# Batch 0: the second state of heads 4 to 7 formed once, and earlier

## The chip, the cores and the metric

The kernel runs on one core of a Trainium2 chip. The metric is the device time of one launch in microseconds, as a median of several runs. A separate execution is recorded by the hardware profiler; its times are those quoted from the profile and the trace.

## The reference

Eight batches of eight heads, 576 positions, head size 64, go through a causal linear attention with a decay for each head (retention); its output of 4608 rows x 512 goes through a feed-forward layer of width 2048 whose activation is h * sigmoid(beta * h).

```python
scores = (1.0 / np.sqrt(D_)) * np.matmul(q, k.transpose(0, 1, 3, 2))
gamma = 1.0 - 2.0 ** (-5.0 - np.arange(H))
Dmat = np.where(rel >= 0, gamma[:, None, None] ** rel[None, :, :], 0.0)   # rel = row - column
ret = np.matmul(scores * Dmat[None], v)
x = ret.transpose(0, 2, 1, 3).reshape(B * S, H * D)
h = x @ w_in
out = (h * (1.0 / (1.0 + np.exp(-beta * h)))) @ w_out
```

The inputs and the output are float32; the matmuls work on bfloat16 copies.

## The kernel before

**Work and tiles.** The first 512 positions of each batch are one block; the last 64 positions of all eight batches together are a ninth block. For each block the attention gives xT, the output transposed (channels on the partitions), then `up` or `ups` forms the 16 pieces of the hidden layer (four matmuls of 128x512 each, and a Silu on ACT into gT), and `down` forms the output rows (16 matmuls of 128x512 for each of four row groups).

**Attention by pieces and states.** The decay is split into a gain on the queries and one on the keys' side, so that within a piece of positions the masked scores times the values give the output, and what comes from earlier pieces is a product of the queries with a state, the sum of keys times values (128x128 for a pair of heads, of which the two 64x64 diagonal blocks count). The matmuls of queries with a state are called cross products.

**Batch 0.** Its 512 positions lie in two spans of 256 (s = 0, 1), each of two pieces of 128: a span's partitions 0 to 63 hold its first piece (`low`) and 64 to 127 its second (`high`). Heads are handled in two halves: a = 0 is heads 0 to 3, a = 1 is heads 4 to 7. The steps are:

- `pre_s`: casts or scales keys and values of a span and a half, on POOL.
- `s_T`: four transposes of the keys (line 470) into a PSUM tile T, and a copy of it by ACT into kT (line 471).
- `s_sc`: 16 score matmuls of 64x64 weights (line 486), then two masks on DVE (line 489) that write R.
- `s_O`: 16 matmuls of R with the values (line 500) into two PSUM tiles of outputs, one for each parity of the piece.
- `s_st(a, n, s, rows, at, fresh)`: state matmuls over the given rows of span s for half a, into bank n of two PSUM banks (tiles `st`). It takes either eight matmuls of 64x64 (line 525) or four of whole pairs of heads (line 531).
- `s_keep(a, n, es, bank, at)`: two casts of a state (lines 540, 542) into `sbds[n]`, the state ahead of piece n + 1, by the engines es. n = 3 keeps the last state in `ends[0]`.
- `s_cross(c, a)`: two cross products of piece c with `sbds[c - 1]` (line 508).
- `s_x(a, hh, e)`: copies one tile of outputs into xT on engine e (line 512).

For heads 4 to 7 the state of span 0 is formed twice, once in each bank: bank 1 becomes the second state and bank 0 is continued with the low rows of span 1 to become the third.

`keep_warm` is a filler: one 128x512 matmul whose result nobody reads. `warm_up` is the same at the start.

**Order.** The kernel's schedule is by hand: each engine executes its instructions in the order in which the program writes them, and semaphores are set by the framework from the tiles that are read and written, for PSUM by whole banks. Slots of a PSUM tag (`mm` 3, `O` 2, `sc` 2, `st` 1) are taken from those that are free.

Ahead of the large products stand the calls of lines 763 to 819. Then `merged` goes through `fill`, a list of large products, and calls the steps of the other streams at the positions in that list that they are given: `rest` (the cross products of heads 4 to 7 and the copies of their outputs) at 1, after the first four products; `last_products` at 2.5; `last_state` at 3.6. Fill's first item is the first half of two hidden pieces, which needs the outputs of heads 0 to 3; its third item needs those of heads 4 to 7.

**Batch 1** works in pieces of 128 too, one step for each (i = 4 to 7): `a_O` outputs, `a_st` state matmuls, `a_cross` cross products, `a_x` the copies to xT, `a_keep` the copies of a state. `second(4)` does these for pieces 4 and 5 near the end of batch 0's `down`. For i = 5 the output lies in two banks, one copied by DVE (line 421), the other by ACT (line 422).

DMAs are issued by SP in the order of the program; the first ones are the queries, keys and values of batch 0, and then the weights. None of the steps that the change touches issues one.

Of the kernel before, what the change touches and what calls it, by code (L numbers as in the profile page):

```python
# [19 lines left out]
def kernel(  # L20
# [10 lines left out]
    nc = tc.nc  # L31
    B, H, S, D = q.shape
# [213 lines left out]
    def keep_warm(tag="mm"):  # L246
        ph = psum.tile([P, CB, P], F32, name="ph", tag=tag, bufs=3 if tag == "mm" else 1)
        nc.tensor.matmul(ph[:], ident[:], ident[:].unsqueeze(1).to_broadcast([P, CB, P]), start=True, stop=True,  # L248
                         skip_group_check=True)
# [16 lines left out]
    def xt(m):  # L266
        if m not in xts:
            xts[m] = xpool.tile([P, HP, CB, P], BF16, name="xT", tag="xT" if m < B else "xTt", bufs=2 if m < B else 1)
        return xts[m]
# [9 lines left out]
    def head_of(b, p, j):  # L279
        return 2 * p + (j if b is not None and b < QB or p < 2 else 1 - j)  # L280
# [49 lines left out]
    def heads(t, p):  # L330
        return t[:, 2 * p:2 * p + 2, :].rearrange("p h d -> p (h d)")
# [27 lines left out]
    def q_cols(i, r, p):  # L359

        b, c = seq[i]
        if b is None:
            return live[i]["qkT"][r, 0, p, :], lambda o: o
        return (batch[b]["qT"][r, :, p, c * PC:(c + 1) * PC], lambda o: o.rearrange("k (i s) -> k i s", i=CB))
# [20 lines left out]
    def new_O(i):  # L385
        tags = ("O", "sc") if split(i) else ("O",)
        live[i]["O"] = [psum.tile([P, 2 if split(i) else HP, P], F32, name="O", tag=t, bufs=2) for t in tags]

    def O_of(i, p):
        Os = live[i]["O"]  # L390
        return Os[p // 2][:, p % 2] if split(i) else Os[0][:, p]

    def opens(i, p):
        return p == 0 or split(i) and p == 2

    def a_cross(i):

        b, c = seq[i]
        for p in range(HP):
            for j in range(2):  # L400
                rhs, view = q_cols(i, half(j), p)
                nc.tensor.matmul(view(O_of(i, p)[half(head_of(b, p, j) % 2)]), sbq[2 * c - 1][half(j), p, :], rhs,
                                 start=False, stop=True, skip_group_check=True)

    def a_O(i):

        b, c = seq[i]
        L = live[i]
        new_O(i)
        R, vn = L["R"], L["vn"]  # L410
        for j, p in [(n % 2, n // 2) for n in range(H)]:
            h = head_of(b, p, j)
            nc.tensor.matmul(O_of(i, p)[half(h % 2)], vn[:, h, :], R[:, j, p, :],
                             start=opens(i, p), stop=c == 0, skip_group_check=True)

    def a_x(i):
        b, c = seq[i]
        x, view = xt(b)[:, :, :, c * PC:(c + 1) * PC], lambda o: o.rearrange("k p (i s) -> k p i s", i=CB)
        Os = live[i]["O"]
        if split(i):  # L420
            nc.vector.tensor_copy(x[:, :2], view(Os[0]))
            nc.scalar.copy(x[:, 2:], view(Os[1]))
        else:
            (nc.scalar.copy if i < E + 2 else nc.vector.tensor_copy)(x, view(Os[0]))

    def a_st(i):

        b, c = seq[i]
        L = live[i]
        if c == 0:  # L430
            state_ps[b] = psum.tile([P, HP, D], F32, name="st", tag="st", bufs=1)
        for p in range(HP):
            for j in range(2):
                nc.tensor.matmul(state_ps[b][half(j), p, :], L["kn"][:, 2 * p + j, :], L["vn"][:, head_of(b, p, j), :],
                                 start=c == 0 and p == 0, stop=True, skip_group_check=True)

    def a_keep(i):

        b, c = seq[i]
        nc.scalar.copy(sbq[2 * c + 1][:], state_ps[b][:])  # L440
        if c:
            nc.vector.tensor_copy(sums[c % 2][:], state_ps[b][:])
# [3 lines left out]
    def half(x):  # L446
        return slice(x * D, (x + 1) * D)

    act, dve = nc.scalar.copy, nc.vector.tensor_copy
# [15 lines left out]
    def s_T(s, a):  # L465
        S = spans[s]
        T = psum.tile([P, 2, 2, P], BF16, name="T", tag="O", bufs=2)
        for i in range(2):
            for pl in range(2):
                nc.tensor.transpose(T[:, i, pl, :], heads(S["kn"][:, i], 2 * a + pl), ident[:])  # L470
        act(S["kT"][:, :, 2 * a:2 * a + 2], T[:])  # L471

    def s_q(c, r, p):
        return batch[0]["qT"][r, :, p, c * PC:(c + 1) * PC]

    def s_view(o):
        return o.rearrange("k (i s) -> k i s", i=CB)
# [13 lines left out]
    s_Os, s_sts = {}, {}  # L491

    def s_O(s, a, tag):

        if s == 0:
            s_Os[a] = [psum.tile([P, 2, 2, P], F32, name="O", tag=tag, bufs=2) for _ in range(2)]
        for i in range(2):
            for pl in range(2):
                for j, hh in spread:
                    nc.tensor.matmul(s_Os[a][hh][half(j), s, pl, :], spans[s]["vn"][half(hh), i, 2 * (2 * a + pl) + j, :],  # L500
                                     spans[s]["R"][a][half(hh), j, i, pl, :], start=s == 0 and i == 0 and pl == 0,
                                     stop=i == 1 and s == 0 and hh == 0, skip_group_check=True)

    def s_cross(c, a):

        for pl in range(2):
            p = 2 * a + pl
            nc.tensor.matmul(s_view(s_Os[a][c % 2][:, c // 2, pl, :]), sbds[c - 1][:, p, :], s_q(c, slice(0, P), p),
                             start=False, stop=True, skip_group_check=True)

    def s_x(a, hh, e):
        e(xt(0)[:, 2 * a:2 * a + 2].rearrange("k p i (s h w) -> k (p i) s h w", s=2, h=2)[:, :, :, hh, :],
          s_Os[a][hh].rearrange("k s p (i w) -> k (p i) s w", i=CB))

    def s_st(a, n, s, rows, at=None, fresh=False):

        if n not in s_sts:
            s_sts[n] = psum.tile([P, HP, P], F32, name="st", tag="mm" if n else "st", bufs=3 if n else 1)
            fresh = True
        S, at = spans[s], 2 * a if at is None else at  # L520
        if a == 0 and rows != whole_span:
            for i in range(2):
                for p in range(2):
                    for j in range(2):
                        nc.tensor.matmul(s_sts[n][half(j), at + p, half(j)], S["kn"][rows, i, 2 * p + j, :],
                                         S["vn"][rows, i, 2 * p + j, :], start=fresh and i == 0 and p == 0, stop=True,
                                         skip_group_check=True)
            return
        for i in range(2):
            for p in range(2):  # L530
                nc.tensor.matmul(s_sts[n][:, at + p, :], heads(S["kn"][rows, i], 2 * a + p), heads(S["vn"][rows, i], 2 * a + p),  # L531
                                 start=fresh and i == 0 and p == 0, stop=True, skip_group_check=True)

    def s_keep(a, n, es, bank=None, at=None):

        ps, at = slice(2 * a, 2 * a + 2), 2 * a if at is None else at
        for j in range(2):
            st = s_sts[min(n, 1) if bank is None else bank][half(j), at:at + 2, half(j)]
            if n < 3:
                es[j](sbds[n][half(j), ps, half(j)], st)  # L540
            else:
                es[j](ends[0][half(1 - j if a else j), ps], st)
# [220 lines left out]
    whole_span, low, high = slice(0, P), half(0), half(1)  # L763
# [11 lines left out]
    keep_warm()  # L775
    pre_s(0, 0, 0)
    s_T(0, 0)
    pre_s(1, 0, 0)
    keep_warm()
    s_sc(0, 0, "sc")  # L780
    s_T(1, 0)
    pre_s(0, 0, 1)
# [17 lines left out]
    s_st(0, 1, 1, low)  # L800
    s_keep(0, 2, (act, act))
    s_O(1, 0, "O")
    s_cross(1, 0)
    s_cross(2, 0)
    s_x(0, 0, act)
    s_cross(3, 0)
    s_x(0, 1, act)
    s_st(1, 1, 0, whole_span)
    s_st(1, 0, 0, whole_span, 0, True)
    s_st(1, 0, 0, low)  # L810
    s_st(1, 0, 1, low, 0)
    s_keep(1, 1, (dve, dve))
    s_keep(1, 0, (dve, dve))
    s_keep(1, 2, (act, act), 0, 0)
    s_O(0, 1, "sc")
    s_O(1, 1, "sc")
    cast_w_in(0, (0, 1), (1,))
# [9 lines left out]
        nc.vector.reciprocal(rbeta_sb[:], beta_sb[:])  # L827

    def last_products():
        s_st(0, 1, 1, high)  # L830
        s_st(1, 1, 1, whole_span)

    def last_state():
        for a in range(2):
            s_keep(a, 3, (dve, dve))

    fill = [F(ups, 0, (fo, fo + 1), u, tags) for u in range(2) for fo, tags in ((0, ("mm", "mm")), (2, ("O", "O")))]
    fill += [F(ups, 0, (4, 5), u, ("sc", "sc")) for u in range(2)]
# [25 lines left out]
    def second(i):  # L864
        a_O(i)
        a_O(i + 1)
        a_st(i + 1)
        a_cross(i + 1)
        a_x(i)
        a_x(i + 1)  # L870
        a_keep(i + 1)
# [78 lines left out]
    for n in range(1, B - 1):  # L950
        lo, hi = (base[n] + 17, base[n + 1] - 9.5) if n == 1 else (base[n] + 3, base[n + 1] - 14)
        at = (lo, hi)
        work = [(n + 1, hi - 0.5, hi + 6)] if n == 1 else [(n + 1, hi - 1, hi + 6.5)]
        if n == B - 2:
            at = (lo, lo + 7, lo + 14, lo + 18)
# [36 lines left out]
```

## Time and profile before

| what | time |
|---|---|
| median of 3 runs | 297.26 us (296.8 to 297.53) |
| the profiled execution itself | 296.29 us |
| its span, first to last instruction | 294.5 us |
| start of the first large product (line 709) | 16.55 us |
| PE busy | 288.4 us, 98% of the span |
| ACT, POOL, DVE busy | 146.1, 112.7, 101.6 us |

In the chain of work that ended last, a line has the start, the length and the instructions of one stretch, in microseconds from the start of the span. In a timeline a line has the start, the length of a group of like instructions up to the end of the last, the engine, the source line, the operation with output and inputs, the shapes, the count, and in brackets how long the engine was idle before and what released it. PEld is the loading of weights on TensorE (PE), which lies beside its matmuls. "issue" is time in which the engine waited for nothing that the profile shows. The end of a matmul is modelled: of two that follow each other, the difference of the starts is what one of them takes.

### The profile page before, as it was taken

To read this page: it belongs to the slowest core of one execution; us is meant where nothing else is said; L and a number is where in the kernel's file an instruction comes from. 1 tells how busy PE (TensorE), PEld (TensorE's weight loads), DVE (VectorE), ACT (ScalarE), POOL (GpSimd) and SP (SyncE) were. 2 spreads that over 40 slices of the span, in tenths; PEclk is the share of its full clock that TensorE was granted. 3 is DMA by queue.
4 is the path that set the end of the run, shared out by engine and by line. 5 is a ranking of instruction groups with operands and counts; after the bars stand their busy time and mean duration, and the time that the engine had idled before them with its cause. 6 is when DMAs were issued, how large, how long until landed. Compare 5 with 4: busy or idle time off the path is not lost.

```text
span 294.5 us, 7957 instructions
## 1 busy us (share of the span) xinstructions
PE 288.4 (98%) x3402; PEld 151.9 (52%) x3402; DVE 101.6 (34%) x216; ACT 146.1 (50%) x260; POOL 112.7 (38%) x227
## 2 busy tenths in 40 slices
PE   7899999999999999999999999999999999999995
PEld 3554477875654454455445544454554544444443
DVE  5764546505630651055204520354053500110012
ACT  5557527892377334743473347434780168007600
POOL 5956037963561914281438216754223000000000
PEclk9999999999999999999999999999999999999999
DMA  7999999999999999939999839999997110131011
GB/s 230 306 366 386 377 231 271 205 180 203 230 217 278 252 163 242 252 63 162 244 257 182 179 106 276 184 174 198 209 167 145 73 38 0 36 71 38 0 71 71
DMA packets 124034, 53.99 MB, mean 183 GB/s; under 512 B 101840, under 2 KB 116448, under 8 KB 124000
## 3 DMA queue, kind: packets, MB, share of 16 engines
q1 hardware_dynamic: 123968, 53.49, 81.3%
q8 instruction: 26, 0.43, 0.6%
q14 instruction: 8, 0.07, 0.1%
q10 hardware_dynamic: 32, 0.01, 0.0%
HBM read 36.71 MB, written 9.44 MB: 157 GB/s over the span
## 4 chain that ended last, share of the span: by engine, by line
PE 95%; DMA 1%; ACT 1%; DVE 1%; issue 0%; DVEq 0%
PE po L729 43%; PE ph L694 38%; PE ph L709 4%; PE st L590 2%; PE O L619 2%; PE sc L572 2%; DMA qn<-in_q_dram 1%; PE O L632 1%; PE T L350 1%; PE st L531 0%; DVE R L489 0%; ACT kT L471 0%; ACT sbd L540 0%; PE sc L486 0%; PE ph L248 0%
## 5 line engine op out<-in xcount | busy, mean ns | idle before, releaser
L729 PE MATMUL po<-w_out_sb,gT 128*128 128x512 bf16 (+3 forms) x640 | 128.9, 358 | 0.0
L696 ACT ACTIVATE gT<-ph,beta_sb 128x512 bf16<-128x512 f32 (+1 forms) x145 | 92.0, 643 | 49.3 <-PE ph L694 48.9
L694 PE MATMUL ph<-xT,w_in_sb 128*128 128x512 bf16 (+1 forms) x580 | 114.5, 357 | 0.0
L729 PEld LDWEIGHTS <-gT 128*128 128x128 bf16 x640 | 60.6, 98 | 60.5
L694 PEld LDWEIGHTS <-w_in_sb 128*128 128x128 bf16 x580 | 56.4, 98 | 55.2 <-DVE first L598 0.5
L736 DVE COPY ot<-po 128x512 f32<-128x512 f32 (+2 forms) x33 | 22.2, 672 | 72.5 <-PE po L729 72.5
L326 POOL CAST kn<-kvn 128x128 bf16<-128x128 f32 (+1 forms) x84 | 24.6, 332 | 45.1 <-DMA kvn<-in_k_dram 45.1
L579 DVE TENSOR_TENSOR R<-sc,tri 128x512 bf16<-128x512 f32 x30 | 18.6, 682 | 59.9 <-PE sc L572 59.9
L297 POOL TENSOR_TENSOR qs<-qn,gq 128x256 bf16<-128x256 f32 (+1 forms) x36 | 26.6, 768 | 33.0 <-DMA qn<-in_q_dram 33.0
L304 POOL TENSOR_TENSOR vn<-kvn,gv 128x512 bf16<-128x512 f32 x28 | 29.1, 1044 | 6.6 <-DMA kvn<-in_v_dram 6.5
L647 ACT CAST xT<-O 128x512 bf16<-128x512 f32 x14 | 7.5, 589 | 31.4 <-PE O L632 31.4
L602 ACT CAST sbd<-warm 128x256 bf16<-128x256 f32 x18 | 7.3, 405 | 25.4 <-DVE warm L598 20.6
L709 PE MATMUL ph<-xT,w_in_sb 128*128 128x512 bf16 x56 | 12.9, 379 | 0.3 <-issue 0.3
L598 DVE TENSOR_TENSOR warm<-st,first 128x256 f32<-128x256 f32 x20 | 8.4, 422 | 10.4 <-PE st L590 9.2
L598 DVE TENSOR_TENSOR first<-st,warm 128x256 f32<-128x256 f32 x25 | 10.6, 425 | 2.9 <-ACT sbd L602 0.5
L314 POOL TENSOR_TENSOR kn<-tln,gq 128x128 bf16<-128x128 f32 (+1 forms) x12 | 5.7, 472 | 14.4 <-PE ph L694 12.0
L712 ACT ACTIVATE gT<-ph,beta_sb 128x512 bf16<-128x512 f32 x14 | 8.6, 687 | 4.6 <-PE ph L709 4.5
L647 DVE CAST xT<-O 128x512 bf16<-128x512 f32 x14 | 9.0, 686 | 4.8 <-PE O L632 4.8
L214 POOL CAST w_in_sb<-wt 128x256 bf16<-128x256 f32 (+1 forms) x15 | 7.6, 526 | 5.0 <-DMA wt<-in_moe_w_in_dram 4.9
L602 ACT CAST sbd<-first 128x256 bf16<-128x256 f32 x18 | 7.3, 405 | 2.7 <-DVE first L598 0.8
L709 PEld LDWEIGHTS <-w_in_sb 128*128 128x128 bf16 x56 | 5.3, 98 | 6.5 <-issue 0.6
L231 DVE TENSOR_SCALAR w_out_sb<-wt,rbeta_sb 128x512 bf16<-128x512 f32 x13 | 5.9, 484 | 5.0 <-DMA wt<-in_moe_w_out_dram 5.0
(119 smaller groups left out, 160.9 us busy)
## 6 DMA issues: line engine op xcount, KB each, us to landing
qn<-in_q_dram SPq DMA_DIRECT2D x16, 512.0 KB, 5.4
kvn<-in_k_dram SPq DMA_DIRECT2D x32, 256.0 KB, 5.8
kvn<-in_v_dram SPq DMA_DIRECT2D x32, 256.0 KB, 5.6
out_dram<-ot SPq DMA_DIRECT2D x31, 256.0 KB, 3.5
wt<-in_moe_w_out_dram SPq DMA_DIRECT2D x8, 512.0 KB, 9.0
wt<-in_moe_w_in_dram SPq DMA_DIRECT2D x5, 512.0 KB, 8.9
wt<-in_moe_w_in_dram SPq DMA_DIRECT2D x6, 256.0 KB, 5.4
tln<-in_q_dram SPq DMA_DIRECT2D x8, 128.0 KB, 4.6
```

What stands on the lines that cost most here:

```text
L297: nc.gpsimd.tensor_tensor(batch[b]["qs"][:, cs, to], q_tiles[b][:, hs, cs].rearrange("p h i d -> p i h d"), gq[:, cs, hs].unsqueeze(3).to_ ...
L304: nc.gpsimd.tensor_tensor(live[i]["vn"], kv_tiles.pop(i)[:, 1], gains(gv, c), ALU.mult)
L326: nc.gpsimd.tensor_copy(kn[:, c % 2, to], t[:, 0, hs])
L579: nc.vector.tensor_tensor(R[x][:, j].rearrange("k c p q -> k (c p) q"), sc[x, j].rearrange("k c p q -> k (c p) q"), mask, ALU.mult)
L598: nc.vector.tensor_tensor(new[:], add, sums[(c - 1) % 2][:], ALU.add)
L602: e((sbq[c] if c < NC - 1 else ends[u])[:], new[:])
L647: (nc.scalar.copy if n % 2 else nc.vector.tensor_copy)(x, o)
L694: nc.tensor.matmul(ph, w_in_sb[:, ko, fo * P:(fo + 1) * P], xts[m][:, ko, :, w], start=(ko == 0), stop=(ko == KO - 1))
L696: nc.scalar.activation(gts[m][:, fo, :, w], ph, ACT.Silu, scale=beta_sb[:, fo:fo + 1])
L709: nc.tensor.matmul(phs[f][:], w_in_sb[:, ko, f * P:(f + 1) * P], xts[m][:, ko], start=(ko == 0), stop=(ko == KO - 1))
L729: nc.tensor.matmul(po[:, x:y], gT[:, fo, ms, :], w_out_sb[:, fo, n0 + x:n0 + y], start=(fo == 0), stop=(fo == FO - 1), skip_group_check=m < 2)
L736: (nc.scalar.copy if m == 0 else nc.vector.tensor_copy)(ot, po[:, :nn])
```

## The change

Five edits:

- The keys' copy of the first `s_T` (span 0, heads 0 to 3) is made in two halves, one by ACT and one by DVE.
- There are two fillers ahead of the first scores in place of one.
- For heads 4 to 7 the whole span 0 is accumulated once, in bank 0, ahead of the cross products of heads 0 to 3, and kept as the second state; the low rows of span 0 go to bank 1 and are kept as the first; bank 0 is continued with the low rows of span 1, and kept as the third. So 12 matmuls take the place of 16. The casts of the first and second states go from DVE to ACT, those of the third from ACT to DVE, and the second copy of the outputs of heads 0 to 3 goes from ACT to DVE.
- The last states are finished in the bank that has the first three pieces, with high rows alone and in the form of eight 64x64 matmuls for both halves.
- In batch 1, the cross products of the second piece come ahead of its state matmuls.

```diff
@@ s_T
                 nc.tensor.transpose(T[:, i, pl, :], heads(S["kn"][:, i], 2 * a + pl), ident[:])
+        if s == a == 0:
+            for i, e in enumerate((act, dve)):
+                e(S["kT"][:, i, 0:2], T[:, i])
+            return
         act(S["kT"][:, :, 2 * a:2 * a + 2], T[:])
@@ s_st
-        if a == 0 and rows != whole_span:
+        if rows == high or a == 0 and rows == low:
...
-                        nc.tensor.matmul(s_sts[n][half(j), at + p, half(j)], S["kn"][rows, i, 2 * p + j, :],
-                                         S["vn"][rows, i, 2 * p + j, :], start=fresh and i == 0 and p == 0, stop=True,
+                        nc.tensor.matmul(s_sts[n][half(j), at + p, half(j)], S["kn"][rows, i, 2 * (2 * a + p) + j, :],
+                                         S["vn"][rows, i, 2 * (2 * a + p) + j, :], start=fresh and i == 0 and p == 0, stop=True,
                                          skip_group_check=True)
@@ calls ahead of the large products
     pre_s(1, 0, 0)
-    keep_warm()
+    for _ in range(2):
+        keep_warm()
     s_sc(0, 0, "sc")
...
     s_O(1, 0, "O")
+    s_st(1, 0, 0, whole_span)
+    s_keep(1, 1, (act, act), 0)
     s_cross(1, 0)
     s_cross(2, 0)
     s_x(0, 0, act)
     s_cross(3, 0)
-    s_x(0, 1, act)
-    s_st(1, 1, 0, whole_span)
-    s_st(1, 0, 0, whole_span, 0, True)
-    s_st(1, 0, 0, low)
-    s_st(1, 0, 1, low, 0)
-    s_keep(1, 1, (dve, dve))
-    s_keep(1, 0, (dve, dve))
-    s_keep(1, 2, (act, act), 0, 0)
+    s_st(1, 1, 0, low)
+    s_x(0, 1, dve)
+    s_keep(1, 0, (act, act), 1)
+    s_st(1, 0, 1, low)
+    s_keep(1, 2, (dve, dve), 0)
     s_O(0, 1, "sc")
     s_O(1, 1, "sc")
@@ last_products, last_state
-        s_st(0, 1, 1, high)
-        s_st(1, 1, 1, whole_span)
+        for a in range(2):
+            s_st(a, 1 - a, 1, high)
...
         for a in range(2):
-            s_keep(a, 3, (dve, dve))
+            s_keep(a, 3, (dve, dve), 1 - a)
@@ second
         a_O(i + 1)
+        a_cross(i + 1)
         a_st(i + 1)
-        a_cross(i + 1)
         a_x(i)
```

## The prediction

> **What bounds the kernel now.** I read the page's busy shares first, then the chain that ended last, then the timeline of PE and of ACT for the first 25 us and for 48 to 50 us, where batch 1's steps stand.
>
> ```profile
> span 294.5 us, 7957 instructions
> PE 288.4 (98%) x3402; PEld 151.9 (52%) x3402; DVE 101.6 (34%) x216; ACT 146.1 (50%) x260; POOL 112.7 (38%) x227
> ```
>
> PE is busy for 98% of the span. The change leaves the large products as they are, so only idle time of PE and its small matmuls can be won. The chain shows where those lie:
>
> ```profile
> 11.67 1.29 DVE R L489 x2
> ...
> 15.04 1.00 PE st L531 x16
> 16.04 0.57 PE O L500 x32
> 16.61 0.97 PE ph L709 x4
> 17.58 0.34 PE O L508 x6
> 17.92 0.22 PE ph L709
> 18.13 0.27 issue
> 18.40 1.69 PE ph L709 x7
> 20.08 0.24 PE st L525 x8
> 20.32 0.33 PE st L531 x4
> ```
>
> The large products start at 16.55 us. Ahead of them stand 16 state matmuls of heads 4 to 7 and then 32 of the outputs. At 18.13 comes a hole that no wait explains. PE's own timeline gives starts:
>
> ```profile
> 14.29 0.76 PE L508 MATMUL O<-qT,sbd 128*128 128x128 bf16 x6
> 14.88 1.16 PE L531 MATMUL st<-vn,kn 128*128 128x128 bf16 x16
> 15.97 0.64 PE L500 MATMUL O<-R,vn 64*64 64x128 bf16 x32
> 16.55 1.04 PE L709 MATMUL ph<-xT,w_in_sb 128*128 128x512 bf16 x4
> 17.42 0.50 PE L508 MATMUL O<-qT,sbd 128*128 128x128 bf16 x6
> 17.75 0.38 PE L709 MATMUL ph<-xT,w_in_sb 128*128 128x512 bf16 x1
> ```
>
> From the timelines of ACT and of all engines, two waits between readers of one PSUM tile: ACT's cast of the third state waited for DVE's casts of the same bank, and in batch 1 DVE's copy of a state waited for ACT's.
>
> ```profile
> 16.76 0.53 ACT L540 CAST sbd<-st 64x128 bf16<-64x128 f32 x2 [0.95 <-DVE sbd L540]
> ...
> 49.68 0.38 PE L356 MATMUL T<-ident,kn 128*128 128x128 bf16 x4 [0.18 <-ACT xT L422]
> ...
> 49.93 0.42 DVE L442 COPY first<-st 128x256 f32<-128x256 f32 x1 [0.31 <-ACT sbd L440]
> ```
>
> **The change part by part.** *First keys' copy and the second filler.* One ACT copy (9.14, 0.59 us) becomes two halves, ACT then DVE. By the two waits just shown, DVE's half starts when ACT's ends. A half takes 0.37 on ACT (128x256 cast, 49.26) and 0.29 on DVE (half the slope between 128x256, 0.42, and 128x512, 0.69). So: 9.14 + 0.37 + 0.05 + 0.29 + 0.05 = 9.90 for the second half's scores, against 9.78 for all of them now. The first eight score matmuls go ahead at 9.56 if PE is free, and eight take 0.14, so the last one starts near 9.97 against 9.98: nothing won. The other end: halves as dear as whole copies (0.59 and 0.69) give 10.52, 0.7 late. I take the first, as the 128x256 rows are the same size. The added filler follows one that starts at 8.89; each holds PE 0.43 there (starts 8.04 to 8.47), so it ends at 9.75, inside the wait for keys. It costs 0 to 0.06, for the change to the smaller tiles. Without that cover it would cost 0.43. What these scores feed is DVE's chain of eight masks, 10.31 to 15.34, whose last one the outputs need at 15.34; PE reaches them later than that in both kernels, so 0.06 is hidden.
>
> *States of heads 4 to 7.* 16 matmuls become 12. They take 15.97 - 14.88 = 1.09, or 0.068 each. Four go ahead of the cross products, at 14.29: their values are ready (POOL's casts of them end by 13.65) and the bank was read by 13.22. Four cross products follow at 14.56 and end their issue by 14.78; the last two waited until 14.76 for ACT anyway (its casts, 14.18 plus 0.53). So these four sit in a hole: +0.02. The next four (low rows, other bank) run 14.90 to 15.17. The last four write the bank that ACT is then reading: its two casts run 14.73 to 15.26 (0.53, as at 14.18), so PE waits until 15.30 and is done at 15.57. Queued behind that wait are only the 32 output matmuls: 0.58 (15.97 to 16.55), so 16.15. They need the last mask, 15.34: there.
>
> The first large product needs both output halves of heads 0 to 3. ACT's goes behind the two state casts: 15.27 to 15.86. DVE's goes behind the last mask: 15.36 to 16.05 (0.69), 16.10 with the handover. PE is there at 16.15, and I take 16.20 for the two waits. Against 16.55: -0.35. The margin to DVE is 0.05 to 0.10. No moved step issues a DMA or goes past POOL's queue; SP's next load waits for a DVE cast behind the second output halves, which comes earlier too.
>
> *Up to the second half of the products.* Four products (0.87) to 17.07, six cross products (0.33) to 17.40. Their states: ACT's casts end by 16.40, DVE's two by 16.65, 0.4 early, against 17.29 now, where PE came at 17.42. The copies of the outputs start at 17.61 and DVE's ends at 18.30. Four products to 18.27; the next, which needs these copies, at 18.35, against 19.05 now (18.40 plus three of 0.216). So -0.70 without the hole. The hole: 17.75 to 18.40 is 0.64 where 0.216 is usual, 0.43 too long. Its releaser is unknown: bounds 0 and, if it grew, below. I take it as staying, so 18.70: -0.35.
>
> The row beside it is one 16 KB instruction fetch, seen between 15.5 and 16 us:
>
> ```profile
> q8 instruction: 1, 0.02, 13.6%
> ```
>
> [...]
>
> *Last states.* 8 + 4 matmuls become 8 + 8 small ones. Now: next product at 20.49, due at 19.92, so 0.57. Eight small ones take 0.12 (20.01 to 20.13), the change to the wide ones 0.12, four wide ones 0.23. After: 0.09 + 0.24 + 0.12 = 0.45, so -0.11. DVE's four casts stay four; they lie beside products.
>
> *Batch 1.* Eight cross products (0.22) go ahead of eight state matmuls (0.22): DVE's half of the outputs comes 0.2 earlier, the state as much later. PE's stop there is at 49.68, for ACT's half, and ACT runs without a gap from 48.27 (0.59, 0.59, 0.37) behind an output copy. So ACT's is not moved: 0. Bounds: -0.18, the whole stop, and +0.2, if ACT's cast of the state at 49.52 came late; it has 0.36 over the matmuls' end at 49.16.
>
> *After that* PE has no stop, and each cast of weights lies 0.8 us or more ahead of its use (queries of batch 1: last at 41.3, needed at 42.1), so the gain is kept.
>
> **Sum.** -0.35 - 0.11 = -0.46 us. The profiled execution took 296.29 (span 294.5, 1.79 around it), so 295.83 on it. It lies 0.97 below the median of 297.26 and below all three runs (296.8 to 297.53). I set the difference against the median: 296.8.
>
> **The rivals.** *B, the hole goes.* As computed, -0.70 - 0.11 = -0.81: 296.45. For it: nothing that the profile shows holds PE there. Against: something did.
>
> *C, the clock comes up sooner.* A filler takes 634 ns at 8.89 and 379 at 10.36, and fillers' starts go from 0.43 to 0.22 apart, while the granted clock reads 1.00 throughout. In a run where that came one group later (scores 0.2, eight transposes at 0.05 more each, a filler 0.21), 0.8 is lost; that would be much of the 0.97 by which the median lies above the profile. More matmuls in the wait could remove it: -0.46 - 0.8, 296.0. Against: PE is nearly full from 5.7 on already.
> [...] The trace has one run only.
>
> *D, slower: the hole widens.* From the fetch (15.5 to 16) to 18.40 are about 2.6 us, of which PE covered 2.2 with work it already had. With fewer matmuls and fewer waits ahead, the cover shrinks. It decides from 0.89 (0.43 + 0.46), and at 2.6 the kernel takes 297.26 + 2.6 - 0.89 = 299.0. [...]
>
> *E, next to no effect.* The hole's end stays at 18.40 and at the same matmul, whatever is done ahead of it: only -0.11 remains, 297.15; or the split delays the first scores by the 0.7 of its bound: DVE's half of the outputs then ends at 16.75, the products start 0.2 late, and with -0.11 it is 297.35. Against the first: where PE has no work left, nothing shows what would hold it to a time.
>
> **How the numbers follow.** Forecast 0.28, B 0.20, C 0.26, D 0.17, E 0.09. 0.3% is 0.89 us, about what a measurement of this kernel can tell from no change: 296.37 and 298.15. C, half of B (its edge is 0.08 off) and 0.05 of the forecast, by the scatter of the runs, are faster: 0.41. The forecast's rest, B's half, E and 0.01 of D are within: 0.43. D's rest: 0.16. The range goes from C's 296.0 less 0.2 to 298.2, inside D. The forecast's own range: 296.4 to 297.2.
>
> **What would show it.** The first large product at 16.2, the seventh to ninth at 18.4 to 18.7, a hole of 0.43 three matmuls later or none, 0.45 for the last states, the stop at 49.7 unchanged. I am wrong if DVE's half of the outputs ends after 16.2, if the first mask starts after 10.4, or if PE stands without a releaser for more than 0.9.

## The result and the profile after

| | before | after |
|---|---|---|
| median of nine runs each | 297.16 us (296.76 to 297.75) | 296.17 us (295.49 to 297.13) |
| the profiled execution, and its span | 296.29, 294.5 us | 296.18, 294.4 us |
| start of the first large product | 16.55 us | 16.29 us |

The ratio is 0.9966 with a 95% interval of 0.995 to 0.9982: a third of a per cent faster, 0.99 us in the medians. The two profiled executions differ by 0.11 us only; the one of before lies 0.87 below its median and the one of after at its own.

PE's timeline of the changed kernel (start, length of the group, engine, line, operation; line 535 has the states of pairs of heads, 529 those of single heads, 713 the large products that come first):

```profile
13.90 0.25 PE L529 MATMUL st<-vn,kn 64*64 64x64 bf16 x4 [0.28 <-ACT sbd L544]
...
14.37 0.40 PE L535 MATMUL st<-vn,kn 128*128 128x128 bf16 x4
14.60 0.52 PE L512 MATMUL O<-qT,sbd 128*128 128x128 bf16 x6
15.05 0.73 PE L535 MATMUL st<-vn,kn 64*128 64x128 bf16 x8
15.72 0.64 PE L504 MATMUL O<-R,vn 64*64 64x128 bf16 x32
16.29 1.04 PE L713 MATMUL ph<-xT,w_in_sb 128*128 128x512 bf16 x4
17.16 0.50 PE L512 MATMUL O<-qT,sbd 128*128 128x128 bf16 x6
17.50 0.81 PE L713 MATMUL ph<-xT,w_in_sb 128*128 128x512 bf16 x3
18.65 1.24 PE L713 MATMUL ph<-xT,w_in_sb 128*128 128x512 bf16 x5 [0.34 <-issue]
19.82 0.44 PE L529 MATMUL st<-vn,kn 64*64 64x64 bf16 x16
20.19 2.76 PE L713 MATMUL ph<-xT,w_in_sb 128*128 128x512 bf16 x12
```

The four matmuls of the second state now run at 14.37 and the six cross products follow without a stop. The first large product starts 0.26 us earlier than before. The hole without a releaser is still there, between 17.93 (the third of the second four products) and 18.65, and 0.50 us too long (0.72 less the usual 0.216) where it was 0.43.

ACT's timeline of the same kernel:

```profile
14.25 1.09 ACT L544 CAST sbd<-st 64x128 bf16<-64x128 f32 x4 [0.41 <-PE st L529]
15.36 0.59 ACT L516 CAST xT<-O 128x512 bf16<-128x512 f32 x1
15.85 0.53 ACT L544 CAST sbd<-st 64x128 bf16<-64x128 f32 x2
```

ACT casts the third state of heads 0 to 3 and then at once the second of heads 4 to 7; its output copy comes after. From DVE's:

```profile
9.59 0.29 DVE L473 COPY kT<-T 128x256 bf16<-128x256 bf16 x1 [0.56 <-ACT kT L473]
...
15.35 0.68 DVE L516 CAST xT<-O 128x512 bf16<-128x512 f32 x1
15.95 0.58 DVE L544 CAST sbd<-st 64x128 bf16<-64x128 f32 x2
```

DVE's half of the first keys waited for ACT's, and took the 0.29 us that were forecast. PE around the first scores and at the two ends of the change, in the kernel before:

```profile
8.89 0.63 PE L248 MATMUL ph<-ident 128*128 128x512 bf16 x1
9.78 0.42 PE L486 MATMUL sc<-qT,kT 64*64 64x128 bf16 x16 [0.25 <-ACT kT L471]
...
13.82 0.25 PE L525 MATMUL st<-vn,kn 64*64 64x64 bf16 x4 [0.29 <-ACT sbd L540]
...
20.49 2.75 PE L709 MATMUL ph<-xT,w_in_sb 128*128 128x512 bf16 x12
```

and in the changed kernel (its third state, at 13.90, and 20.19 are above):

```profile
8.94 0.99 PE L248 MATMUL ph<-ident 128*128 128x512 bf16 x2
9.87 0.42 PE L490 MATMUL sc<-qT,kT 64*64 64x128 bf16 x16
```

The filler that both kernels have starts 0.05 us later here, ahead of anything that the change touches. The first scores follow the second filler without a stop and start 0.09 later, the third state 0.08. At the other end the first product behind the last states comes 0.30 us earlier (20.49 to 20.19), but from there to the end of the span this execution takes 0.20 us longer (274.25 against 274.05); that is how the two spans come to differ by 0.1 only.

### The profile page after: what moved, and what is told of

Its sections match the earlier page's. It is cut to its first block, busy times and chain, and to the rows that moved or that the text cites. A ratio compares the mean times of both kernels' runs of the same rounds, so it can differ in the third digit from the quotient of the medians.

```text
span 294.4 us, 7961 instructions
## 1 busy us (share of the span) xinstructions
PE 288.7 (98%) x3403; PEld 151.9 (52%) x3403; DVE 101.9 (35%) x216; ACT 145.8 (50%) x261; POOL 112.6 (38%) x227
## 4 chain that ended last, share of the span: by engine, by line
PE 95%; DMA 1%; ACT 1%; DVE 1%; issue 0%; DVEq 0%
PE po L733 43%; PE ph L698 38%; PE ph L713 4%; PE sc L576 2%; PE st L594 2%; PE O L623 2%; DMA qn<-in_q_dram 1%; PE O L636 1%; PE T L350 1%; PE ph L248 1%; DVE R L493 0%; PE st L535 0%; PE T L356 0%; PE O L504 0%; PE sc L490 0%
```

## The experiments

Two views carry them: the ratio of the times, and stretches of the profile. The second is the sharper. I use three stretches, each the difference of two starts on PE: from the third state of heads 0 to 3 to the first large product (the states of heads 4 to 7 lie in it); from there to the first product of the third four (cross products, the output copies and the hole); and from there to the first product behind the last states. The ratio is the one on record, to the kernel before on the same chip; it is not the quotient of the two medians and lies up to 0.001, or 0.3 us, from it (no_split: 296.35 to 296.91 would be 0.9981). All columns behind it are in us; "third state" and "first product" are starts. The theories that the expectations name by letters are explained there, each at its first use.

| kernel | ratio, 95% interval | third state | first product | stretch 1 | stretch 2 | stretch 3 | span |
|---|---|---|---|---|---|---|---|
| before | | 13.82 | 16.55 | 2.73 | 2.51 | 1.43 | 294.5 |
| before_again | 1.0006 (0.999 to 1.0021) | 13.74 | 16.46 | 2.72 | 2.34 | 1.44 | 294.5 |
| head | 1.0015 (1.0 to 1.0031) | 14.42 | 17.14 | 2.72 | 2.54 | 1.43 | 295.3 |
| before_late | 1.0001 (0.9984 to 1.0018) | 14.20 | 16.92 | 2.72 | 2.56 | 1.43 | 295.6 |
| after | 0.9966 (0.995 to 0.9982) | 13.90 | 16.29 | 2.39 | 2.58 | 1.33 | 294.4 |
| after_again | 0.998 (0.9967 to 0.9994) | 14.01 | 16.44 | 2.43 | 2.25 | 1.32 | 294.2 |
| states | 0.9983 (0.9967 to 0.9998) | 14.51 | 16.90 | 2.39 | 2.38 | 1.34 | 294.9 |
| one_filler | 0.9994 (0.9981 to 1.0007) | 13.94 | 16.33 | 2.39 | 2.57 | 1.34 | 294.6 |
| no_split | 0.9991 (0.9978 to 1.0003) | 14.01 | 16.40 | 2.39 | 2.24 | 1.33 | 294.1 |
| batch1_back | 0.9981 (0.9968 to 0.9994) | 14.54 | 16.93 | 2.39 | 2.32 | 1.32 | 295.2 |
| after_early | 0.9981 (0.9967 to 0.9995) | 13.62 | 16.01 | 2.39 | 2.65 | 1.33 | 294.3 |
| after_late | 0.9982 (0.9966 to 0.9999) | 14.39 | 16.78 | 2.39 | 2.25 | 1.32 | 294.4 |
| after_pairs | 0.9995 (0.9979 to 1.0011) | 14.68 | 17.27 | 2.59 | 2.25 | 1.32 | 295.3 |
| after_order | 1.0005 (0.999 to 1.002) | 14.36 | 17.33 | 2.97 | 2.25 | 1.32 | 295.3 |

Stretch 1 is 2.72 or 2.73 in all four profiles with the old states, 2.39 in seven of the eight that have the new ones as the change makes them, and 2.43 in the eighth. Stretch 3 is 1.43 or 1.44 and 1.32 to 1.34. These two are the change: -0.33 and -0.10 us. What is left, from the first product behind the last states to the end of the span, does not tell the kernels apart: 274.05 to 274.71 us in the four, 274.07 to 274.61 in the eight, with means of 274.31 and 274.26.

Of the ratios, those of one_filler, no_split, after_pairs and after_order have intervals that hold 1. So for single edits the times decide little, and the stretches decide.

**The kernel before once more.** No edit.

> The kernel before, unchanged. It shows how far two profiled executions of one kernel differ, and what the runs scatter by. Theory S (the states' matmuls are the gain): its profile has the first large product at 16.5 +- 0.1 us and the end at 294.5 +- 0.3, and the medians agree within 0.2 us. Theory C (in most runs the clock comes up later than in the profile of before): its large products start later than 16.55 us, or its fillers at 10.4 still take 0.63 us, and the end lies at 295 or above.

Measured: 296.81 us against 296.80, and runs from 295.95 to 297.74. The profiled execution has the same span as the first one, 294.5, and yet another start. PE's timeline:

```profile
8.61 0.38 PE L248 MATMUL ph<-ident 128*128 128x512 bf16 x1
9.45 0.42 PE L486 MATMUL sc<-qT,kT 64*64 64x128 bf16 x16 [0.46 <-ACT kT L471]
```

The filler at 8.61 takes 0.38 us where the one at 8.89 took 0.63: in this execution the clock was up several microseconds earlier (the trace's record of the clock has it from 5.47 us on, and from 9.69 in the first profile). Theory S's three figures are met (the first product is at 16.46). Theory C's form, that most executions are later than the profile, is not what this shows; that the clock's step falls differently from run to run is.

**The states alone.** The edits to `s_T`, to the fillers and to batch 1 are left out:

```diff
-        if s == a == 0:
-            for i, e in enumerate((act, dve)):
-                e(S["kT"][:, i, 0:2], T[:, i])
-            return
...
-    for _ in range(2):
-        keep_warm()
+    keep_warm()
...
-        a_cross(i + 1)
         a_st(i + 1)
+        a_cross(i + 1)
```

> Only the states of heads 4 to 7 and the last states are changed; first keys' copy, fillers and batch 1 as before. Theory S: the first large product at 16.2 to 16.3 us and the whole gain, -0.7 to -1.0 us in the medians. Theory C: the same start, but the medians gain only 0.3 to 0.5 us, as the second filler is missing. The hole of 0.43 us stands one matmul further on than in the changed kernel, since one filler (two instructions of PE) less is ahead of it, if it belongs to a place in PE's code.

Measured: 296.26 against 296.80, -0.54 us. The median lies between the two forecasts, nearer to C's. But stretches 1 and 3 have the whole of their gain without the second filler. The hole stands behind the fourth product (18.76 to 19.29), one matmul further on than in the changed kernel, as expected. (Part of these 0.53 us is the wait for the output copies: where there is no hole, the same two starts are 0.39 apart.) In this execution the clock came up late (the filler at 9.40 still takes 0.63 us): the first scores are at 10.28, and the first product at 16.90 in spite of the shorter stretch.

**The head alone.** The kernel before with these two edits:

```diff
+        if s == a == 0:
+            for i, e in enumerate((act, dve)):
+                e(S["kT"][:, i, 0:2], T[:, i])
+            return
...
-    keep_warm()
+    for _ in range(2):
+        keep_warm()
```

> The kernel before with only the two halves of the first keys' copy and the second filler. Theory S: no gain, 0 to +0.1 us, the first mask 0.1 later as in the changed kernel. Theory C: the medians gain 0.4 to 0.8 us.

Measured: 297.29 against 296.80, a ratio of 1.0015 (1.0 to 1.0031). C's 0.4 to 0.8 us of gain are not there. The profile shows how much the clock can cost. Stretches of time of this execution (length; busy time of PE, PEld, DVE, ACT and POOL with the count of instructions; then the granted clock of PE, the share of the DMA engines and what they moved in GB/s):

```profile
4.30:7.60 3.30, 1.97 (x15) 0.86 (x14) 2.59 (x4) 1.72 (x4) 1.70 (x4) 1.00 1.08 320
7.70:11.00 3.30, 3.30 (x32) 2.01 (x33) 1.29 (x3) 0.37 (x1) 2.68 (x4) 0.50 1.17 291
11.10:16.00 4.90, 4.34 (x125) 3.08 (x122) 4.61 (x9) 3.79 (x11) 4.82 (x9) 1.00 1.12 327
```

The granted clock was 1.00 while PE was busy for 1.97 of 3.30 us, and in the next 3.30 us it was 0.50 while PE was busy without a break. The third state starts at 14.42 in place of 13.82. Seven of the twelve executions had such a loss by their mean granted clock (0.995 or less), against 8 of 35 of the kernel before on this chip; among the others the span still averages 295.26 against 294.91, so the edits of the head gain nothing there either. The trace's record of the clock has 0.50 from 7.66 to 11.07 us, 3.41 us. In the 3.30 us ahead of it PE was 60% busy; what lowered the clock is not shown.

**One filler.** The changed kernel with

```diff
-    for _ in range(2):
-        keep_warm()
+    keep_warm()
```

> The changed kernel with one filler ahead of the first scores. Theory S: the same time as the changed kernel within 0.2 us, -0.9 against before, first scores no later. Theory C: 0.4 to 0.8 us of the gain are lost, -0.2 to -0.5 against before.

Measured: 296.42 against 296.80, -0.38 us, which is in C's range and not in S's. But no_split and states, below and above, are as near to it as to the changed kernel, and the head alone, which has the second filler, gained nothing, so I don't take this median for C. The interval of its ratio, 0.9981 to 1.0007, holds 1 and ends next to the 0.998 of the changed kernel's repeat, so the times don't decide it. In the profile stretch 1 is whole, and between the fourth product and the next (18.18 to 18.90) PE stands 0.50 us too long, one matmul further on than in the changed kernel; part of that, as in states, is the wait for the output copies.

**The changed kernel once more,** on another chip with the next three. No edit.

> The changed kernel, unchanged, beside its own variants on one chip. Theory P (the gain is PE's order of states, some 0.3 to 0.5 us, and the rest of the measured 1.0 is where the clock's steps fell in the runs): -0.3 to -0.6 us against before, with a scatter of 1.5 us as before has, since a late or a lost clock step costs 0.6 to 1.0 in single runs. Theory C (the second filler makes the clock come up sooner): -0.9 to -1.0 again.

Measured: 296.29 against 296.91, -0.62 us, a ratio of 0.998 (0.9967 to 0.9994): at the edge of P's range, and less than the 0.99 of the first nine runs. The hole among the second products is not there, in the same kernel that showed it above; stretch 2 is 2.25, which is what the output copies allow.

**Batch 1 as before.**

```diff
-        a_cross(i + 1)
         a_st(i + 1)
+        a_cross(i + 1)
```

> The changed kernel with batch 1's order as before. Theory P: the time of the changed kernel within 0.2 us, and PE's stop of 0.18 us before the second pair of transposes (at 49.1 to 49.7) is back. In the changed kernel that stop was not there, so 0.1 to 0.2 us may be lost. A rival, that the order of batch 1 carries the gain, loses 0.4 or more.

Measured: 296.34, as after_again. From batch 1's first output matmul to the next large product are 1.73 us in the changed kernel (47.87 to 49.60), and 1.74 here (48.25 to 49.99) and before (48.16 to 49.90). The stop with a releaser is back, but it had not been won: in the changed kernel the first four transposes start 1.06 us behind that output matmul (48.93) and here 0.94 (49.19), and PE then waits for the same ACT copy in both, from the fourth transpose to the fifth 0.27 us there (49.11 to 49.38, the copy ends at 49.33) and 0.40 here (49.37 to 49.77, 49.72). The edit is worth nothing here.

**The first keys' copy whole.**

```diff
-        if s == a == 0:
-            for i, e in enumerate((act, dve)):
-                e(S["kT"][:, i, 0:2], T[:, i])
-            return
```

> The changed kernel with the first keys' copy by ACT alone. Theory P: within 0.2 us of the changed kernel; first mask at 10.3 to 10.4 where the clock is up by 9.8, and the first large product at 16.2 to 16.3. If the halves were the gain, 0.3 or more is lost and the first mask starts 0.1 to 0.3 later than in the changed kernel.

Measured: 296.35, within 0.1 of after_again in the medians. All its stretches are those of after_again or of the changed kernel. The first mask starts at 10.12, 0.28 earlier than in the changed kernel's first profile.

**One more filler early.** The changed kernel with

```diff
     betas()
+    keep_warm()
     betas_safe()
```

> The changed kernel with one more filler behind the turning of beta, where PE waits for the queries (5.25 to 5.65 us). If the scatter of the runs is the clock's, and more matmuls hold it, fewer runs have a mean granted clock of 0.995 or less, and the median is 0.2 to 0.6 below the changed kernel's. If the filler changes nothing for the clock, the time is the same or up to 0.1 us longer, and the share of such runs stays.

Measured: 296.12, 0.17 below after_again in the medians, but with the same ratio (0.9981 and 0.998): the 0.2 to 0.6 were not met, and no gain is shown. None of its twelve executions had a mean granted clock of 0.995 or less (an estimate from head: its 3.41 us at 0.50 in 295 take 0.006 off the mean); of after_again's twelve five had, of the kernel before's 35 on that chip seven. For the clock the direction is the expected one; the numbers are small.

The same runs show how much longer such executions are: the spans of those seven executions of the kernel before average 295.87 us, those of the other 28 294.95. For after_again it is 294.84 (five) and 294.36 (seven).

**States of pairs.** The changed kernel with the condition of `s_st` cut:

```diff
-        if rows == high or a == 0 and rows == low:
+        if rows == high:
```

> The changed kernel with the first and third states of heads 0 to 3 as four matmuls of pairs of heads each, in place of eight of single heads: 16 instructions of PE fewer ahead of the large products. Theory F (the hole is the wait for one block of PE's code, at a fixed place in it, ending 2.4 to 2.8 us after the fetch starts): the place moves eight matmuls on, into the last states at 19.0 to 19.3 us, where PE comes after the fetch is there, so the hole shrinks or goes, the ninth large product starts at 18.4 to 18.6 in place of 18.87, and the median is 0.2 to 0.4 us below the changed kernel's. If the hole belongs to the matmul (a wait on its operands), it stays behind the third product of the second four, 0.4 to 0.5 long, and the time stays.

Measured: the hole behind the third product is gone. PE's timeline:

```profile
17.27 1.04 PE L713 MATMUL ph<-xT,w_in_sb 128*128 128x512 bf16 x4
...
18.48 2.06 PE L713 MATMUL ph<-xT,w_in_sb 128*128 128x512 bf16 x8
```

The eight products run from 18.48 with one short wait, ahead of the fifth at 19.52, for the output copies that end at 19.37. (The mean granted clock of this execution was 0.993, as in head's profile, and the starts are later than forecast.) A missing hole is what theory F asked for, but this one does not show F: the changed kernel itself had no hole in after_again either. And the gain that F expected is not there; the kernel is not even shown to be faster than the one before, 0.9995 (0.9979 to 1.0011). Its stretch 1 is 2.59, 0.20 longer. That lies in the third state of heads 0 to 3, now four wide matmuls: from its start to the second state of heads 4 to 7 it is 0.68 us (14.68 to 15.36) against 0.47 in the changed kernel (13.90 to 14.37).

**Without the first warm-up matmuls,** the kernel before (before_late) and the changed one (after_late):

```diff
-    warm_up(2, MB)
```

> [...] Theory K (what the runs scatter by is when the clock comes up): its mean is 0.3 to 1.0 us above the kernel before's, and no profile shows the clock up by 5.5. If the clock's time does not matter, it is as fast as the kernel before within 0.2 us.

> The changed kernel without the first warm-up matmuls. Theory K with a gain that is larger where the clock comes late: 0.8 or more below the kernel before with the same omission. If the gain doesn't depend on the clock: 0.3 to 0.6 below it. Theory C (the second filler brings the clock up sooner) also expects 0.8 or more, and the clock up one step (3.4 us) sooner in the profile than in that kernel.

Measured: 297.14 for before_late, 0.14 above the kernel before's median on that chip (297.00); 296.30 for after_late, 0.84 below before_late. In the trace's record of the clock it comes up at 9.9 us in the first and at 11.2 in the second, so in these two executions the second filler did not bring it up sooner. None of the 24 executions had a mean granted clock of 0.995 or less; an early clock that is lost again, as in head, was not seen without the early matmuls. K's first expectation, a mean 0.3 or more above, was not met: the means are 297.13 and 297.04. A gain of 0.84 is what K's second half and C asked for; by the ratios (1.0001 and 0.9982) it is 0.56, and would be on the other side, so this is not decided. The three stretches of the two profiles give 0.33, 0.31 and 0.11, together 0.75, while the third state started 0.19 later in the profile of after_late; 0.64 more of the difference of the two spans lies behind the last states, where before_late has the longest rest of all (274.71).

**The order of the states.** The changed kernel with

```diff
-    s_st(1, 0, 0, whole_span)
-    s_keep(1, 1, (act, act), 0)
     s_cross(1, 0)
     s_cross(2, 0)
     s_x(0, 0, act)
     s_cross(3, 0)
+    s_st(1, 0, 0, whole_span)
+    s_keep(1, 1, (act, act), 0)
```

> The changed kernel with the four matmuls of the second state, and its two casts, behind the cross products of heads 0 to 3 in place of ahead of them; still 12 matmuls. From the third state's first matmul of heads 0 to 3 to the first large product the profiles show 2.72 us with the old states and 2.39 with the new. If the fewer matmuls are the gain (four of 0.068), this stretch is 2.4 to 2.5 and the time that of the changed kernel. If their place ahead, and with it the early cast that the third state waits for, is the gain: ACT casts the second state behind its output copy, at 15.4 to 15.9, PE waits for that, and the stretch is 2.7 to 3.0, with the whole gain of 0.33 lost.

Measured: 296.92 against 296.94, 1.0005 (0.999 to 1.002): the whole gain is gone, with 12 matmuls as in the changed kernel. PE's timeline:

```profile
14.83 0.76 PE L512 MATMUL O<-qT,sbd 128*128 128x128 bf16 x6
15.42 0.71 PE L535 MATMUL st<-vn,kn 128*128 128x128 bf16 x8
16.43 0.39 PE L535 MATMUL st<-vn,kn 64*128 64x128 bf16 x4 [0.30 <-ACT sbd L544]
16.75 0.64 PE L504 MATMUL O<-R,vn 64*64 64x128 bf16 x32
17.33 1.04 PE L713 MATMUL ph<-xT,w_in_sb 128*128 128x512 bf16 x4
```

and ACT's:

```profile
15.27 0.58 ACT L516 CAST xT<-O 128x512 bf16<-128x512 f32 x1
15.84 1.09 ACT L544 CAST sbd<-st 64x128 bf16<-64x128 f32 x4
```

ACT makes its output copy first and casts the second state from 15.84 on, and PE's next state matmuls start only at 16.43, when those two casts are done. Stretch 1 is 2.97, 0.25 longer than in the kernel before. The place ahead of the cross products, and with it the early cast, carries the gain; four matmuls fewer do not show without it. The reverse, the early place with 16 matmuls, was not run, so what the four add to it stays open.

## Why the prediction was right

It forecast -0.46 us and a time of 296.8; measured were -0.99 and 296.17. That is inside the stated range, which reaches down to 295.8 for the sake of rival C, but 0.23 below the forecast's own range of 296.4 to 297.2 and nearer to C's 296.0, whose reason the runs did not bear out. The forecast of "within 0.3%" had the larger chance by a little, and it came out just faster than that. So the first time hit the range with some luck. The mechanism and its size are better borne out than that time: the seven other sets of runs with the new states as the change makes them have ratios of 0.998 to 0.9994, on average 0.9985, which is -0.46 us. By its steps:

- *States of heads 4 to 7: -0.35.* Measured -0.33 in stretch 1, in seven of the eight profiles, and -0.29 in the eighth. The placing in PE's hole, ACT's two casts between, and PE's wait for them came as worked out (the casts end at 15.34, PE goes on at 15.39); DVE's half of the outputs ended at 16.03, forecast 16.05.
- *Last states: -0.11.* Measured -0.10.
- *First keys and second filler: 0 to 0.06, hidden.* The size came as forecast, the hiding failed. With the clock's step at much the same place (9.69 and 9.74 us) the first scores moved from 9.78 to 9.87, and the third state from 13.82 to 13.90. Of these, 0.05 stood there before the edit (8.89 to 8.94), so the edit cost some 0.03 to 0.04, and it was not hidden. The first mask started at 10.40, just at the limit that the prediction had set itself. I looked at what the scores feed through the masks; the way that counts goes through PE, ACT's next copies of keys, the next scores and the states behind them. The head alone was at least no faster than the kernel before (1.0015, 1.0 to 1.0031).
- *Batch 1: 0.* Measured 1.73 and 1.74 us for the same work.
- *The hole: taken as staying, three matmuls further on.* It stayed in the profile of the changed kernel, at 0.50 for 0.43, two matmuls further on: I had not counted a wait instruction that the new order of the states adds to PE's code; the trace of the changed kernel has it at 16.07, that of the kernel before has none there. In the nine profiles that show the hole its place follows the number of PE's instructions ahead of it: behind product 1 of the second four in the kernel before, ahead of it with one filler more, behind product 3 in the changed kernel, behind 4 with one filler less, behind 2 with one more. In all nine, before_late included, 448 or 449 of PE's records in the trace (matmuls, weight loads and waits) lie ahead of it. Its length varies: stretch 2 is 2.24 or 2.25 where there is none and 2.32 to 2.65 where there is one. In the five profiles without a hole PE comes to that place 2.4 to 3.9 us after the start of the 16 KB fetch; in the nine with one it would, at its usual pace, have come there after 1.9 to 2.6.
- *The 16 KB fetch.* That PE waits for the fetch of one block is inferred from the hole's fixed place and from the times above; no run changed the fetch itself, and after_pairs, where the place was moved, can't show it, as the hole can be gone without that. The forecast's "three matmuls later" took the place to follow the count of PE's instructions, which no trace had shown when it was made; the profiles put the hole two matmuls later, with 448 or 449 records ahead of it.
- *Rival C, the clock.* The row that it rested on is real: the record of the clock begins at 5.47 us in one profile of the kernel before and at 9.69 in the other, and in head it was back at 0.50 for 3.41 us. But that more matmuls in the wait bring the clock up sooner, and with it the 0.8 of C's sum, was my assumption, and no run shows it: the head alone gained nothing (C's 0.4 us would be a ratio of 0.9987, outside its interval), and after_late's clock was no earlier than before_late's (11.2 and 9.9 us), in one profile each. So C is out as a cause of the change's gain.
- *Rival B, the hole goes.* It stayed in the first profile and was gone in the repeat of the same kernel, so both happen; where it is gone stretch 2 is 0.33 us shorter (2.58 and 2.25). The hole shows in all four profiles of the old states and in five of the eight of the new.
- *Rivals D and E.* The hole did not widen by more than 0.15 us. D's cover of 2.2 us took the hole to be a wait for the fetch, which is not shown. The fetch itself started 0.34 us later in the changed kernel's profile (15.73 to 16.07), though the first product was 0.26 earlier. E's fixed end was not seen: in after_early the products started at 16.01, 0.28 earlier than in the changed kernel, and the hole ended at 18.23 in place of 18.65. Nor did the halves reach their dear bound.

The sum in the profiles is -0.33 - 0.10 + 0.03, or -0.40. Stretch 2 averages 2.49 in the four profiles of the old states and 2.41 in the eight of the new, -0.08, less than its scatter; with it the sum is -0.48. The step that was off in the result is the last one, setting a difference of two traces against a median. In further runs the medians differ by 0.62 (after_again), 0.54 (states) and 0.84 (after_late against before_late), and the ratios, with their -0.46 on average, agree with the stretches. So what stays open is the -0.99 of the first nine runs, whose interval ends at -0.53. Scatter of the medians is the plain reading, not a shown one. One more candidate is the clock: executions in which it was lost were longer by 0.62 to 0.92 us in the kernel before on four chips and by 0.99 in states, which has the old head, but by -0.37 to 0.58 in the seven kernels with one or both edits of the head (two to seven such executions each). That points to the head under half the clock, but it wasn't taken apart.

## What to carry to other kernels

In a start-up where PE, ACT and DVE hand each other small pieces, the place of a product can count for more than the number of matmuls, as it did here: put a state ahead of work that waits anyway, so that its cast is done before the next writer of that bank needs it. Measure such a change by a stretch between two fixed instructions of the profile, which here repeated to 0.04 us while single executions of one kernel scattered by some 1.5. And follow an operation's result along every engine before calling its delay hidden.

## What the runs showed of the hardware

- Two executions of one kernel had PE at a different pace in the same work: a 128x512 filler took 0.63 us at 8.89 in one profile of the kernel before and 0.38 at 8.61 in the other, and the record of the clock begins at 9.69 and at 5.47 us. Where the clock was lost once more (head), it was granted at 0.50 from 7.66 to 11.07 us. In the seven executions of the kernel before on one chip with a mean granted clock of 0.995 or less the span was 0.92 us longer than in the other 28 (295.87 and 294.95).
- PE's hole without a releaser sat at one place of its code in the nine profiles that show it, behind 448 or 449 of its recorded instructions, whichever product stood there; the stretch around it took 2.24 or 2.25 us without a hole and 2.32 to 2.65 with one. The next matmul started 2.4 to 2.9 us after the start of a 16 KB instruction fetch in eight of these nine (2.67 in the kernel before, 2.58 in the changed one), and 3.1 in one.
- Without the first warm-up the kernel before was not measurably slower (a ratio of 1.0001, 0.9984 to 1.0018), and none of its 12 executions had a mean granted clock of 0.995 or less.
